# K and V tiles of 2 MB with two kv heads, one on each half of the partitions, in place of 1 MB tiles with one head

## The chip, the cores and the metric

One core of one Trainium2 chip runs one launch of the kernel. The metric is the device time of that launch in microseconds (us). The four runs of the kernel before lie within 0.2% (403.78 to 404.50 us). Where runs of one kernel differ by more than 1.5%, the slower ones count as "slow" and are not compared with fast ones.

## The reference

It is one decode step of a transformer block, batch 4. Layer norm and a query projection come first. Then attention of 32 query heads over the last 4,096 positions of a cache with 16 kv heads, an output projection, and a gated feed-forward layer. All arrays are bf16.

```
W = 4096                                            # the window, of Sk = 16384
q = layernorm(x) @ wq                               # 4 x 32 heads x 128
k, v = k_cache[:, :, Sk-W:, :], v_cache[:, :, Sk-W:, :]     # 4 x 16 x 4096 x 128
p = softmax(q k^T / sqrt(128));  o = p v
h = x + o @ wo
gate = layernorm(h) @ W_gate;  up = layernorm(h) @ W_up
out = h + (relu(gate) * up) @ W_down
```

K and V of the windows are 2 x 4 x 16 x 1 MiB = 134.2 MB. The weights add 25 MB. So the kernel reads about 160 MB and has little arithmetic for it. One head's window is 1 MiB without a gap, and the next head's window starts 4 MiB further on (16,384 x 128 x 2 bytes).

## The kernel before

A tile is one head's window of K or V, 128 partitions x 8 KB: partition p holds 32 successive positions. All large transfers go through one queue, issued by SyncE, into 16 slots. A slot is loaded again when the last reader of its tile is done.

```python
def add_kv(kind, i):
    b, kvh = divmod(i, KVH)
    s = ring_slot()
    off = slot0 + s * TILE
    src = (A_k_cache if kind == "K" else A_v_cache)[b, kvh, SK - WIN:SK, :].rearrange("(p t) d -> p (t d)", p=128)
    place((kind, i), off, TILE, ("TR", i) if kind == "K" else ("PV", i),
          lambda e: e.dma_start(out=arena[:, off:off + TILE], in_=src), key=f"slot{s}")
```

PE transposes each K tile (32 transposes, L373), VectorE and ScalarE copy it out of PSUM, and PE multiplies it with q (L402). After 16 heads come the exponential and the transposes of P (8, L425). Then each V tile is multiplied with P (L452). The P of each head stands in its own columns of `pTm`, with zeros beside it.

Of the kernel before, what the change touches and what calls it, by code (L numbers as in the profile page):

```python
# [11 lines left out]
B = 4  # L12
D = 576
H = 32
KVH = 16
# [4 lines left out]
DC = 5  # L20
NPAIR = B * KVH
SCALE = DH ** -0.5
EPS = 1e-5

NKT = 3
NSLOT = 16
TILE = 4096
QLAG = 2
VDMA_LAG = KVH + 2
PV_LAG = KVH + 3  # L30
# [90 lines left out]
def bass_sequential_preLN__sliding_block_cached__glu_gated_reglu__decode_kernel(  # L121
# [12 lines left out]
    with ExitStack() as es:  # L134
# [11 lines left out]

        arena = sb("arena", [128, (NKT + NSLOT) * TILE], BF16)
        pTm = sb("pTm", [128, 8, 4, KVH, 32], BF16)
        ident_b = sb("ident_b", [128, 128], BF16)
# [33 lines left out]

        kT = [arena[:, i * TILE:(i + 1) * TILE] for i in range(NKT)]
        slot0 = NKT * TILE

# [24 lines left out]

        ring = [(-DC - 2 * NPAIR) % NSLOT]

        def ring_slot():
            s = ring[0] % NSLOT
            ring[0] += 1
            return s

        def add_kv(kind, i):
            b, kvh = divmod(i, KVH)  # L220
            s = ring_slot()
            off = slot0 + s * TILE
            src = (A_k_cache if kind == "K" else A_v_cache)[b, kvh, SK - WIN:SK, :].rearrange("(p t) d -> p (t d)", p=128)
            place((kind, i), off, TILE, ("TR", i) if kind == "K" else ("PV", i),
                  lambda e: e.dma_start(out=arena[:, off:off + TILE], in_=src), key=f"slot{s}")  # L225

        def add_wq(c):
            s = ring_slot()
            off = slot0 + s * TILE
            w = _dw(c)  # L230
            place(("wq", c), off, TILE, "QMM",
                  lambda e: e.dma_start(out=arena[0:w, off:off + H * DH], in_=A_wq[c * 128:c * 128 + w, :]), key=f"slot{s}")  # L232

        P.dma("scalar", ("L", "x"), lambda e: e.dma_start(out=x_bf[:, :], in_=A_x.rearrange("b s d -> (b s) d")), "d_x")
        for s in range(2):
            add_kv("K", s)
        for c in range(DC):
            add_wq(c)
        for s in range(2, NPAIR):
            add_kv("K", s)  # L240
            if s >= VDMA_LAG:
                add_kv("V", s - VDMA_LAG)
        for i in range(NKT):
            for blk in range(i * TILE // 64, (i + 1) * TILE // 64):
                owner[blk] = "QKEND"
# [3 lines left out]
        WDJ = 9 * D  # L249
        rest = list(range(NPAIR - VDMA_LAG, NPAIR))  # L250
        for n, v in enumerate(rest):
            add_kv("V", v)
            if n == len(rest) - 7:
                place(("wo",), WO_OFF, H * D, "WO",
                      lambda e: e.dma_start(out=arena[:, WO_OFF:WO_OFF + H * D].rearrange("p (h n) -> p h n", n=D),
                                            in_=A_wo.rearrange("(h p) n -> p h n", p=128)))
# [16 lines left out]
        def kv(kind, i):  # L273
            off = land[(kind, i)]
            return arena[:, off:off + TILE].rearrange("p (t d) -> p t d", d=DH)
# [38 lines left out]

        tpv = bankb[6]

        def pe_q():
            for c in range(DC):
                w = _dw(c)
                pe(None, lambda e, c=c, w=w: e.transpose(out=tpv[0:w, c * 4:(c + 1) * 4], in_=xn_bf[0:B, c * 128:c * 128 + w],  # L320
                                                         identity=ident_b[0:B, 0:B]), ["xn", "c_idb"] if c == 0 else [])
# [4 lines left out]
            for c in range(DC):  # L326
                w = _dw(c)
                off = land[("wq", c)]
                for n in range(8):
                    g, bk = n % 4, n // 4  # L330
                    pe("QMM", lambda e, c=c, w=w, off=off, n=n, g=g, bk=bk: e.matmul(  # L331
                        bank[4 + bk][32 * g:32 * g + 32, :], lhsT=xnT[0:w, c, :], rhs=arena[0:w, off + n * 512:off + (n + 1) * 512],
                        start=(c == 0), stop=(c == DC - 1), skip_group_check=True),
                        ([("L", "wq", c)] + (["xnT", "c_xnT"] if c == 0 else [])) if n == 0 else [])
            for bk in range(2):
# [24 lines left out]
        def pe_tr(i):  # L360
            kn = kv("K", i)
            for j in range(4):
                for u in range(8):
                    t = j * 8 + u
                    deps = []
                    if u == 0:
                        deps = [("L", "K", i)] if j == 0 else []
                        if i == 0:
                            deps.append("c_idb")
                        else:  # L370
                            deps.append(("EV", i - 1, j))
# [17 lines left out]
        def pe_qk(i):  # L389
            b, kvh = divmod(i, KVH)  # L390
            k = kT[i % NKT]
            for u in range(2):
                for j in range(4):
                    deps = []
                    if u == 0:
                        deps.append(("EV", i, j))
                    if j == 0 and kvh == 0:
                        if b == 0:
                            deps += ["qTm", "qev0", "qev1"]
                        else:  # L400
                            deps += [("EXP", b - 1), ("MAX", b - 1)]
                    o = pe(("QK", i), lambda e, u=u, j=j: e.matmul(  # L402
                        bank[4 + u][32 * j:32 * j + 32, :], lhsT=qTm[:, b, kvh, :],
                        rhs=k[:, j * 1024 + u * 512:j * 1024 + (u + 1) * 512],
                        start=(kvh == 0), stop=(kvh == KVH - 1), skip_group_check=True), deps)
            if i == NPAIR - 1:
                P.names["QKEND"] = o
# [7 lines left out]
        def act_exp(b):  # L415
            act(("EXP", b), lambda e: e.activation(out=p_sb[:, :], in_=s_ps, func=ACT.Exp, bias=stat[:, b, 1:2], scale=SCALE,  # L416
                                                   accum_out=stat[:, b, 2:3]),
                [("NB", b), ("PT", b - 1) if b else ("QT", 7)])

        def pe_pt(b):  # L420
            for tl in range(8):
                deps = []
                if tl == 0:
                    deps = [("EXP", b), ("ONORM", b - 1) if b else "qTm"]
                pe(("PT", b), lambda e, tl=tl: e.transpose(out=mb_ps[:, tl * 128:(tl + 1) * 128],  # L425
                                                           in_=p_sb[:, tl * 128:(tl + 1) * 128], identity=ident_b[:, :]), deps)

        def put_pT(b):
            for half in range(2):
                dst = bass.AP(tensor=pTm, offset=half * 4 * 4 * KVH * 32,  # L430
                              ap=[[8 * 4 * KVH * 32, 128], [KVH * 32, 16], [34, KVH], [1, 2]])
                src = mb_ps[:, half * 512:(half + 1) * 512].rearrange("p (a k h) -> p a k h", k=KVH, h=2)
                deps = [("PT", b), "c_pTm"]
                if b:
                    deps.append(("PV", b * KVH - 1))
                if half == 0:
                    dve(("PM", b, 0), lambda e, dst=dst, src=src: e.tensor_copy(out=dst, in_=src), deps)
                else:
                    dve(("PM", b, 1), lambda e, dst=dst, src=src: e.tensor_copy(out=dst, in_=src), deps)

        def pe_pv(i):
            b, kvh = divmod(i, KVH)
            v = kv("V", i)
            for tl in range(8):
                for j in range(4):
                    deps = []
                    if tl == 0 and j == 0:
                        deps.append(("L", "V", i))
                        if kvh == 0:
                            deps += [("PM", b, 0), ("PM", b, 1)]  # L450
                            deps.append(("OEV", b - 1) if b else "xT")
                    pe(("PV", i), lambda e, tl=tl, j=j: e.matmul(  # L452
                        o_ps[32 * j:32 * j + 32, 0:DH], lhsT=pTm[:, tl, j, kvh, :], rhs=v[:, 8 * j + tl, :],
                        start=(kvh == 0 and tl == 0), stop=(kvh == KVH - 1 and tl == 7), skip_group_check=True), deps)


        def weights(b):
            pe(("MT", b), lambda e: e.matmul(m_ps[0:1, 0:128], lhsT=stat[:, b, 0:1], rhs=ident_f[:, :], start=True, stop=True),
               [("MAX", b), ("PM", b, 0), ("PM", b, 1), "c_idf"])
            dve(("GM", b), lambda e: e.tensor_reduce(out=gm4[0:1, 0:32], in_=m_ps[0:1, 0:128].rearrange("p (j h) -> p h j", j=4),  # L460
# [23 lines left out]
        for s in range(NPAIR + PV_LAG):  # L484
            if s >= PV_LAG and (s - PV_LAG) % KVH == 0:
                pe_pt((s - PV_LAG) // KVH)
                put_pT((s - PV_LAG) // KVH)
            if s < NPAIR:
                pe_tr(s)
                for j in range(4):  # L490
                    evac(s, j)
            if s == 1:
                pe_q()
# [137 lines left out]
```

## Time and profile before

| | before |
|---|---|
| time, median of 4 runs | 404.08 us (403.78 to 404.50) |
| K and V bytes | 134.2 MB in 128 transfers of 1 MB |
| rate while K and V stream | 419 GB/s |
| PE, VectorE, ScalarE busy | 66%, 30%, 34% |

These are lines of the profile's page of the kernel before. First come the span and the engines' busy time in us, with the share of the span and the instructions. Then rows of the span in 40 equal slices (busy tenths, and GB/s). Part 3 has a row for each DMA queue: packets, MB and share of 16 engines. Part 4 is the chain of waits that ended last. The L lines give busy us, mean ns of one, and idle time before them with what ended it. The last lines give count, KB and us from issue to landing.

```profile
span 402.3 us, 10840 instructions
...
PE 265.4 (66%) x5091; PEld 209.7 (52%) x5091; DVE 121.9 (30%) x218; ACT 138.3 (34%) x154; POOL 3.9 (1%) x21
...
DMA  8999999999999999999999999999999999999992
GB/s 321 372 402 422 419 419 419 419 418 421 419 418 421 419 420 419 421 419 418 419 420 419 420 419 420 416 421 419 421 419 419 412 367 370 425 422 415 209 360 118
...
## 3 DMA queue, kind: packets, MB, share of 16 engines
q1 hardware_dynamic: 25104, 159.59, 98.2%
...
q10 hardware_dynamic: 24, 0.01, 0.0%
...
## 4 chain that ended last, share of the span: by engine, by line
DMA 67%; PE 19%; SPq 9%; DVE 3%; issue 1%; ACT 0%
...
L373 PE MATMUL psb<-sb_ident_b,sb_arena 128*128 128x128 bf16 x2048 | 151.9, 243 | 60.4 <-DMA sb_arena<-in_A_k_cache_dram 53.8
...
L452 PE MATMUL psb<-sb_arena,sb_pTm 128*32 128x128 bf16 x2048 | 49.2, 251 | 32.7 <-DMA sb_arena<-in_A_v_cache_dram 31.5
...
sb_arena<-in_A_k_cache_dram SPq DMA_DIRECT2D x64, 1024.0 KB, 27.9
sb_arena<-in_A_v_cache_dram SPq DMA_DIRECT2D x64, 1024.0 KB, 27.6
```

The DMA row is full in nearly every slice, and the GB/s row stays near 419. The two PE groups spend their idle time waiting for K and V transfers. So the data queue is the limit, and PE (66% busy) follows it.

A transfer of n rows here makes n packets for its data and, as the counts below come out, one more for each DMA engine that took part (an inference; no view names the engines). In the packet records of the trace file, which no view lists, these extra packets have 4 bytes: 2,389 of them in this kernel. Queue q10 moved x and half of the output: three transfers of 4 rows, 24 packets. That is 3 x (4 + 4), so four engines took part in each. On q1, 25,104 is the sum over all its transfers if each large one is counted with 16 engines and each of the two outputs with 4 (K and V: 128 x (128 + 16) = 18,432; all others 6,672). The column "DMA share", which a view by windows gives as the mean busy share of the core's 16 engines, bears this reading out for K and V: in the stretch shown below it is 1.01. Texts call the extra packets completions.

The stretch from 40 to 305 us, from the view by windows (us; busy us of PE, PE's weight loads, VectorE, ScalarE and GpSimd; granted clock; DMA share; GB/s):

```profile
core 0: us, PE busy (x) PEld busy (x) DVE busy (x) ACT busy (x) POOL busy (x), PEclk, DMA share, GB/s
40.00:305.00 265.00, 205.63 (x4015) 168.30 (x4016) 97.54 (x162) 122.41 (x131) 0.00 (x0) 0.88 1.01 419
```

And two V tiles from the end of the V stage, in the timeline (start us, duration us, what, and in brackets the idle time before and what ended it). Tiles of 1 MB come 2.48 us apart:

```profile
348.73 1.04 PE L452 MATMUL psb<-sb_arena,sb_pTm 128*32 128x128 bf16 x32 [1.44 <-DMA sb_arena<-in_A_v_cache_dram]
351.21 1.05 PE L452 MATMUL psb<-sb_arena,sb_pTm 128*32 128x128 bf16 x32 [1.44 <-DMA sb_arena<-in_A_v_cache_dram]
```

### The profile page before, as it was taken

The numbers are of one execution on the slowest core, as the hardware profiler recorded it, in microseconds if no ns is written. First come the engines' busy times: TensorE is split into PE (matmuls) and PEld (weight loads), VectorE is DVE, ScalarE is ACT, GpSimd is POOL, SyncE is SP. The second block draws the span as 40 slices with busy tenths as digits, with TensorE's granted clock in tenths as the row PEclk, the third lists the DMA queues.
The fourth block names the chain that finished last, engine by engine and source line by source line (L and its number), as shares of the span: only waits on it lengthen the run. The fifth ranks groups of instructions, "written<-read, shape, count | busy, mean of one in ns | idle before, by whom it ended". The sixth has DMA issues, their size and how long they took to land.

```text
span 402.3 us, 10840 instructions
## 1 busy us (share of the span) xinstructions
PE 265.4 (66%) x5091; PEld 209.7 (52%) x5091; DVE 121.9 (30%) x218; ACT 138.3 (34%) x154; POOL 3.9 (1%) x21
## 2 busy tenths in 40 slices
PE   4555999988777776867776767877774420465253
PEld 4244777766566655656564656666653320342022
DVE  4147555643222243422222433322232000011020
ACT  4222777754333353434333532533330100000010
POOL 3000000000000000000000000000000000000000
PEclk9866999999888889888889897988886555566556
DMA  8999999999999999999999999999999999999992
GB/s 321 372 402 422 419 419 419 419 418 421 419 418 421 419 420 419 421 419 418 419 420 419 420 419 420 416 421 419 421 419 419 412 367 370 425 422 415 209 360 118
DMA packets 25172, 160.29 MB, mean 398 GB/s; under 512 B 2404, under 2 KB 6504, under 8 KB 6504
## 3 DMA queue, kind: packets, MB, share of 16 engines
q1 hardware_dynamic: 25104, 159.59, 98.2%
q8 instruction: 40, 0.66, 0.7%
q10 hardware_dynamic: 24, 0.01, 0.0%
q14 instruction: 4, 0.03, 0.0%
HBM read 159.58 MB, written 0.00 MB: 397 GB/s over the span
## 4 chain that ended last, share of the span: by engine, by line
DMA 67%; PE 19%; SPq 9%; DVE 3%; issue 1%; ACT 0%
DMA sb_arena<-in_A_k_cache_dram 42%; PE psb L373 13%; DMA sb_arena<-in_A_v_cache_dram 11%; DMA sb_arena<-in_B_W_down_dram 10%; SPq L225 8%; DMA sb_arena<-in_A_wq_dram 4%; PE psb L402 3%; DVE sb_pTm L496 2%; PE psb L452 1%; PE psb L518 1%; SPq L232 1%; PE psb L593 0%; DVE sb_stat L410 0%; ACT sb_p_sb L416 0%; PE psb L331 0%
## 5 line engine op out<-in xcount | busy, mean ns | idle before, releaser
L373 PE MATMUL psb<-sb_ident_b,sb_arena 128*128 128x128 bf16 x2048 | 151.9, 243 | 60.4 <-DMA sb_arena<-in_A_k_cache_dram 53.8
L373 PEld LDWEIGHTS psb<-sb_ident_b,sb_arena 128*128 128x128 bf16 x2048 | 140.1, 111 | 74.2 <-DMA sb_arena<-in_A_k_cache_dram 60.2
L387 ACT COPY sb_arena<-psb 128x1024 bf16<-128x1024 bf16 x128 | 125.4, 1014 | 143.2 <-PE psb L373 143.2
L385 DVE COPY sb_arena<-psb 128x1024 bf16<-128x1024 bf16 x128 | 87.9, 690 | 152.0 <-PE psb L373 151.7
L452 PE MATMUL psb<-sb_arena,sb_pTm 128*32 128x128 bf16 x2048 | 49.2, 251 | 32.7 <-DMA sb_arena<-in_A_v_cache_dram 31.5
L452 PEld LDWEIGHTS psb<-sb_arena,sb_pTm 128*32 128x32 bf16 x2048 | 41.6, 113 | 50.7 <-DMA sb_arena<-in_A_v_cache_dram 35.5
L402 PE MATMUL psb<-sb_arena,sb_qTm 128*32 128x512 bf16 x512 | 44.0, 425 | 1.0 <-ACT sb_p_sb L416 1.0
L560 PE MATMUL psb<-sb_arena,sb_hnT 128*32 128x384 bf16 (+1 forms) x120 | 10.2, 500 | 14.8 <-DMA sb_arena<-in_B_W_up_dram 8.4
L523 ACT COPY sb_pTm<-psb 128x288 f32<-128x288 f32 x1 | 0.4, 398 | 46.4 <-PE psb L518 46.4
L478 DVE COPY sb_o_sb<-psb 128x128 f32<-128x128 f32 x4 | 1.2, 291 | 45.2 <-PE psb L452 45.2
L560 PEld LDWEIGHTS psb<-sb_arena,sb_hnT 128*32 128x32 bf16 (+1 forms) x120 | 4.0, 130 | 20.4 <-DMA sb_arena<-in_B_W_up_dram 10.4
L402 PEld LDWEIGHTS psb<-sb_arena,sb_qTm 128*32 128x32 bf16 x512 | 8.1, 97 | 9.0 <-issue 3.3
L564 ACT ACTIVATE sb_pTm<-psb 128x384 f32<-128x384 f32 x3 | 1.3, 492 | 23.9 <-PE psb L560 23.9
L567 DVE TENSOR_TENSOR sb_pTm<-psb,sb_pTm 128x384 bf16<-128x384 f32 x3 | 1.5, 550 | 24.0 <-ACT sb_pTm L564 24.0
L331 PE MATMUL psb<-sb_arena,sb_xnT 128*32 128x512 bf16 (+1 forms) x40 | 3.9, 478 | 6.8 <-DMA sb_arena<-in_A_wq_dram 6.4
L496 DVE MEMSET sb_pTm<- 128x8192 uint32 x1 | 6.9, 6885 | 1.6 <-issue 1.6
L593 PE MATMUL psb<-sb_arena,sb_pTm 128*32 128x144 bf16 x144 | 3.9, 277 | 4.2 <-DMA sb_arena<-in_B_W_down_dram 4.2
L416 ACT ACTIVATE sb_p_sb<-psb,sb_stat 128x1024 bf16<-128x1024 f32 x4 | 4.5, 1114 | 6.2 <-DVE sb_stat L412 6.2
L410 DVE TENSOR_REDUCE sb_stat<-psb 128x1 f32<-128x1024 f32 x4 | 4.9, 1225 | 4.3 <-PE psb L402 4.3
L468 ACT ACTIVATE sb_stat<-sb_stat 128x1 f32<-128x1 f32 x4 | 0.8, 203 | 14.5 <-DVE sb_stat L466 14.5
L593 PEld LDWEIGHTS psb<-sb_arena,sb_pTm 128*32 128x32 bf16 x144 | 3.2, 121 | 4.8 <-DMA sb_arena<-in_B_W_down_dram 4.6
L331 PEld LDWEIGHTS psb<-sb_arena,sb_xnT 128*32 128x32 bf16 (+1 forms) x40 | 0.7, 99 | 9.2 <-DMA sb_arena<-in_A_wq_dram 8.7
(94 smaller groups left out, 64.7 us busy)
## 6 DMA issues: line engine op xcount, KB each, us to landing
sb_arena<-in_A_k_cache_dram SPq DMA_DIRECT2D x64, 1024.0 KB, 27.9
sb_arena<-in_A_v_cache_dram SPq DMA_DIRECT2D x64, 1024.0 KB, 27.6
sb_arena<-in_B_W_down_dram SPq DMA_DIRECT2D x4, 1296.0 KB, 36.5
sb_arena<-in_A_wo_dram SPq DMA_DIRECT2D x1, 4608.0 KB, 31.7
sb_arena<-in_B_W_gate_dram SPq DMA_DIRECT2D x4, 1152.0 KB, 27.0
sb_arena<-in_B_W_up_dram SPq DMA_DIRECT2D x4, 1152.0 KB, 28.4
sb_arena<-in_A_wq_dram SPq DMA_DIRECT2D x4, 1024.0 KB, 11.2
sb_arena<-in_B_W_gate_dram SPq DMA_DIRECT2D x1, 576.0 KB, 33.5
```

Of the source, the lines that this page charges most:

```text
L225: lambda e: e.dma_start(out=arena[:, off:off + TILE], in_=src), key=f"slot{s}")
L331: pe("QMM", lambda e, c=c, w=w, off=off, n=n, g=g, bk=bk: e.matmul(bank[4 + bk][32 * g:32 * g + 32, :], lhsT=xnT[0:w, c, :], rhs=arena[0:w ...
L373: o = pe(("TRJ", i, j), lambda e, j=j, u=u, t=t: e.transpose(out=bankb[TRB[j]][:, u * 128:(u + 1) * 128], in_=kn[:, t, :], identity=ident_ ...
L385: dve(("EV", i, j), lambda e: e.tensor_copy(out=dst, in_=src), deps)
L387: act(("EV", i, j), lambda e: e.copy(out=dst, in_=src), deps)
L402: o = pe(("QK", i), lambda e, u=u, j=j: e.matmul(bank[4 + u][32 * j:32 * j + 32, :], lhsT=qTm[:, b, kvh, :], rhs=k[:, j * 1024 + u * 512:j ...
L410: dve(("MAX", b), lambda e: e.tensor_reduce(out=stat[:, b, 0:1], in_=s_ps, axis=AX.X, op=ALU.max, negate=True), [("QK", b * KVH + KVH - 1)])
L416: act(("EXP", b), lambda e: e.activation(out=p_sb[:, :], in_=s_ps, func=ACT.Exp, bias=stat[:, b, 1:2], scale=SCALE, accum_out=stat[:, b, 2 ...
L452: pe(("PV", i), lambda e, tl=tl, j=j: e.matmul(o_ps[32 * j:32 * j + 32, 0:DH], lhsT=pTm[:, tl, j, kvh, :], rhs=v[:, 8 * j + tl, :], start= ...
L496: dve("c_pTm", lambda e: e.memset(pflat, 0.0))
L560: pe(("GU", c), lambda e, c=c, w=w, g=g, m=m, j=j, lo=lo: e.matmul(bank[3 * g + m][32 * j:32 * j + 32, 0:384], lhsT=hnT[0:w, c, :], rhs=ar ...
L593: pe("DOWN", lambda e, j=j, r=r, n=n, wv=wv: e.matmul(bank[0][32 * n:32 * n + 32, 0:144], lhsT=hhT[:, r * 128 + 32 * j:r * 128 + 32 * j + 32],
```

## The change

The intent: longer runs in memory (16 KB in place of 8 KB), half as many transfers and completions. A tile of 2 MB holds two heads. Head 0 lies on partitions 0 to 63, head 1 on 64 to 127, each with 64 positions (16 KB) per partition. P must then lie on both halves: it is transposed twice, and each half keeps only its head's columns. The wq chunks move to 2 MB tiles as well. Its core, with cuts marked:

```diff
-NSLOT = 16
-TILE = 4096
+NSLOT = 8
+TILE = 8192
...
         def add_kv(kind, i):
-            b, kvh = divmod(i, KVH)
+            b, k2 = divmod(i, BT)
...
-            src = (A_k_cache if kind == "K" else A_v_cache)[b, kvh, SK - WIN:SK, :].rearrange("(p t) d -> p (t d)", p=128)
+            cache = A_k_cache if kind == "K" else A_v_cache
+            src = cache[b, 2 * k2:2 * k2 + 2, SK - WIN:SK, :].rearrange("a (p t) d -> a p (t d)", p=64)
...
-                        rhs=k[:, j * 1024 + u * 512:j * 1024 + (u + 1) * 512],
+                        bank[4 + u][32 * j:32 * j + 32, :], lhsT=qTm[:, b, 2 * k2 + a, :], rhs=k[:, j, :, a, :],
...
-                pe(("PT", b), lambda e, tl=tl: e.transpose(out=mb_ps[:, tl * 128:(tl + 1) * 128],
-                                                           in_=p_sb[:, tl * 128:(tl + 1) * 128], identity=ident_b[:, :]), deps)
+                for a in range(2):
+                    pe(("PT", b, r), lambda e, tl=tl, a=a: e.transpose(out=mb_ps[64 * a:64 * a + 64, tl * 128:(tl + 1) * 128],
+                                                                       in_=p_sb[:, (r * 8 + tl) * 64:(r * 8 + tl + 1) * 64],
+                                                                       identity=ident_b[:, :]), deps if a == 0 else [])
...
+            for a in range(2):
+                dst = bass.AP(tensor=pTm, offset=64 * a * 16384 + r * 8192 + 2 * a, ap=[[16384, 64], [256, 32], [36, BT], [1, 2]])
```

More of the change, by code (lines that the diff above doesn't have):

```diff
@@ L21 @@
 NPAIR = B * KVH
+NTILE = NPAIR // 2
+BT = KVH // 2
 SCALE = DH ** -0.5
@@ L25 @@
 NKT = 3
-NSLOT = 16
-TILE = 4096
+NSLOT = 8
+TILE = 8192
+UNIT = 4096
 QLAG = 2
-VDMA_LAG = KVH + 2
+VDMA_LAG = BT + 1
 PV_LAG = KVH + 3
@@ L144, in bass_sequential_preLN__sliding_block_cached__glu_gated_reglu__decode_kernel @@
         pool = lambda name, fn, deps=(): P.op("gpsimd", name, fn, deps)
-        arena = sb("arena", [128, (NKT + NSLOT) * TILE], BF16)
-        pTm = sb("pTm", [128, 8, 4, KVH, 32], BF16)
+        arena = sb("arena", [128, NKT * UNIT + NSLOT * TILE], BF16)
+        pTm = sb("pTm", [128, 16, 4, BT, 32], BF16)
         ident_b = sb("ident_b", [128, 128], BF16)
@@ L182, in bass_sequential_preLN__sliding_block_cached__glu_gated_reglu__decode_kernel @@
         hhT = pflat[:, 4608:4608 + 1152]
-        kT = [arena[:, i * TILE:(i + 1) * TILE] for i in range(NKT)]
-        slot0 = NKT * TILE
+        kT = [arena[:, i * UNIT:(i + 1) * UNIT] for i in range(NKT)]
+        slot0 = NKT * UNIT
         psb = es.enter_context(nc.psum_tensor("psb", [128, 8, 512], FP32))
@@ L210, in place @@
             land[name] = off
-        ring = [(-DC - 2 * NPAIR) % NSLOT]
+        ring = [(-3 - 2 * NTILE) % NSLOT]
         def ring_slot():
@@ L219, in add_kv, with add_wq @@
         def add_kv(kind, i):
-            b, kvh = divmod(i, KVH)
+            b, k2 = divmod(i, BT)
             s = ring_slot()
             off = slot0 + s * TILE
-            src = (A_k_cache if kind == "K" else A_v_cache)[b, kvh, SK - WIN:SK, :].rearrange("(p t) d -> p (t d)", p=128)
-            place((kind, i), off, TILE, ("TR", i) if kind == "K" else ("PV", i),
+            cache = A_k_cache if kind == "K" else A_v_cache
+            src = cache[b, 2 * k2:2 * k2 + 2, SK - WIN:SK, :].rearrange("a (p t) d -> a p (t d)", p=64)
+            place((kind, i), off, TILE, ("TR", 2 * i + 1) if kind == "K" else ("PV", 2 * i + 1),
                   lambda e: e.dma_start(out=arena[:, off:off + TILE], in_=src), key=f"slot{s}")
-        def add_wq(c):
+        wq_off = []
+        def add_wq(m):
             s = ring_slot()
             off = slot0 + s * TILE
-            w = _dw(c)
-            place(("wq", c), off, TILE, "QMM",
-                  lambda e: e.dma_start(out=arena[0:w, off:off + H * DH], in_=A_wq[c * 128:c * 128 + w, :]), key=f"slot{s}")
-        P.dma("scalar", ("L", "x"), lambda e: e.dma_start(out=x_bf[:, :], in_=A_x.rearrange("b s d -> (b s) d")), "d_x")
-        for s in range(2):
-            add_kv("K", s)
-        for c in range(DC):
-            add_wq(c)
-        for s in range(2, NPAIR):
+            if m < 2:
+                wq_off.extend([off, off + H * DH])
+                src = A_wq[m * 256:(m + 1) * 256, :].rearrange("(p r) n -> p (r n)", r=2)
+                place(("wq", m), off, TILE, "QMM", lambda e: e.dma_start(out=arena[:, off:off + TILE], in_=src), key=f"slot{s}")
+            else:
+                wq_off.append(off)
+                place(("wq", m), off, TILE, "QMM",
+                      lambda e: e.dma_start(out=arena[0:64, off:off + H * DH], in_=A_wq[512:576, :]), key=f"slot{s}")
+        P.dma("scalar", ("L", "x"), lambda e: e.dma_start(out=x_bf[:, :], in_=A_x.rearrange("b s d -> (b s) d")), "d_x")
+        add_kv("K", 0)
+        for m in range(3):
+            add_wq(m)
+        for s in range(1, NTILE):
             add_kv("K", s)
@@ L243, in bass_sequential_preLN__sliding_block_cached__glu_gated_reglu__decode_kernel @@
         for i in range(NKT):
-            for blk in range(i * TILE // 64, (i + 1) * TILE // 64):
+            for blk in range(i * UNIT // 64, (i + 1) * UNIT // 64):
                 owner[blk] = "QKEND"
@@ L249, in bass_sequential_preLN__sliding_block_cached__glu_gated_reglu__decode_kernel @@
         WDJ = 9 * D
-        rest = list(range(NPAIR - VDMA_LAG, NPAIR))
+        rest = list(range(NTILE - VDMA_LAG, NTILE))
         for n, v in enumerate(rest):
             add_kv("V", v)
-            if n == len(rest) - 7:
+            if n == len(rest) - 4:
                 place(("wo",), WO_OFF, H * D, "WO",
@@ L273, in kv @@
         def kv(kind, i):
-            off = land[(kind, i)]
+            off = land[(kind, i // 2)]
             return arena[:, off:off + TILE].rearrange("p (t d) -> p t d", d=DH)
@@ L315, in bass_sequential_preLN__sliding_block_cached__glu_gated_reglu__decode_kernel @@
         tpv = bankb[6]
+        xn_rows = lambda c: (xn_bf[0:B, 512:576] if c == 4 else
+                             xn_bf[0:B, c // 2 * 256:c // 2 * 256 + 256].rearrange("b (p r) -> b r p", r=2)[:, c % 2, :])
         def pe_q():
@@ L319, in pe_q @@
                 w = _dw(c)
-                pe(None, lambda e, c=c, w=w: e.transpose(out=tpv[0:w, c * 4:(c + 1) * 4], in_=xn_bf[0:B, c * 128:c * 128 + w],
+                pe(None, lambda e, c=c, w=w: e.transpose(out=tpv[0:w, c * 4:(c + 1) * 4], in_=xn_rows(c),
                                                          identity=ident_b[0:B, 0:B]), ["xn", "c_idb"] if c == 0 else [])
@@ L327, in pe_q @@
                 w = _dw(c)
-                off = land[("wq", c)]
+                off = wq_off[c]
                 for n in range(8):
@@ L333, in pe_q @@
                         start=(c == 0), stop=(c == DC - 1), skip_group_check=True),
-                        ([("L", "wq", c)] + (["xnT", "c_xnT"] if c == 0 else [])) if n == 0 else [])
+                        ([("L", "wq", c // 2)] + (["xnT", "c_xnT"] if c == 0 else [])) if n == 0 and c % 2 == 0 else [])
             for bk in range(2):
@@ L363, in pe_tr @@
                 for u in range(8):
-                    t = j * 8 + u
+                    t = j * 16 + i % 2 * 8 + u
                     deps = []
                     if u == 0:
-                        deps = [("L", "K", i)] if j == 0 else []
+                        deps = [("L", "K", i // 2)] if j == 0 else []
                         if i == 0:
@@ L389, in pe_qk @@
         def pe_qk(i):
-            b, kvh = divmod(i, KVH)
-            k = kT[i % NKT]
-            for u in range(2):
+            dp, u = divmod(i, 2)
+            b, k2 = divmod(dp, BT)
+            k = kT[i % NKT].rearrange("p (j t a k) -> p j t a k", j=4, t=8, a=2)
+            for a in range(2):
                 for j in range(4):
                     deps = []
-                    if u == 0:
+                    if a == 0:
                         deps.append(("EV", i, j))
-                    if j == 0 and kvh == 0:
+                    if j == 0 and k2 == 0:
                         if b == 0:
@@ L401, in pe_qk @@
                             deps += [("EXP", b - 1), ("MAX", b - 1)]
-                    o = pe(("QK", i), lambda e, u=u, j=j: e.matmul(
-                        bank[4 + u][32 * j:32 * j + 32, :], lhsT=qTm[:, b, kvh, :],
-                        rhs=k[:, j * 1024 + u * 512:j * 1024 + (u + 1) * 512],
-                        start=(kvh == 0), stop=(kvh == KVH - 1), skip_group_check=True), deps)
+                    o = pe(("QK", i), lambda e, a=a, j=j: e.matmul(
+                        bank[4 + u][32 * j:32 * j + 32, :], lhsT=qTm[:, b, 2 * k2 + a, :], rhs=k[:, j, :, a, :],
+                        start=(k2 == 0 and a == 0), stop=(k2 == BT - 1 and a == 1), skip_group_check=True), deps)
             if i == NPAIR - 1:
@@ L417, in act_exp, with pe_pt @@
                                                    accum_out=stat[:, b, 2:3]),
-                [("NB", b), ("PT", b - 1) if b else ("QT", 7)])
-        def pe_pt(b):
+                [("NB", b), ("PT", b - 1, 1) if b else ("QT", 7)])
+        def pe_pt(b, r):
             for tl in range(8):
@@ L423, in pe_pt, with put_pT @@
                 if tl == 0:
-                    deps = [("EXP", b), ("ONORM", b - 1) if b else "qTm"]
-                pe(("PT", b), lambda e, tl=tl: e.transpose(out=mb_ps[:, tl * 128:(tl + 1) * 128],
-                                                           in_=p_sb[:, tl * 128:(tl + 1) * 128], identity=ident_b[:, :]), deps)
-        def put_pT(b):
-            for half in range(2):
-                dst = bass.AP(tensor=pTm, offset=half * 4 * 4 * KVH * 32,
-                              ap=[[8 * 4 * KVH * 32, 128], [KVH * 32, 16], [34, KVH], [1, 2]])
-                src = mb_ps[:, half * 512:(half + 1) * 512].rearrange("p (a k h) -> p a k h", k=KVH, h=2)
-                deps = [("PT", b), "c_pTm"]
+                    deps = [("PM", b, 0, 0), ("PM", b, 0, 1)] if r else [("EXP", b), ("ONORM", b - 1) if b else "qTm"]
+                for a in range(2):
+                    pe(("PT", b, r), lambda e, tl=tl, a=a: e.transpose(out=mb_ps[64 * a:64 * a + 64, tl * 128:(tl + 1) * 128],
+                                                                       in_=p_sb[:, (r * 8 + tl) * 64:(r * 8 + tl + 1) * 64],
+                                                                       identity=ident_b[:, :]), deps if a == 0 else [])
+        def put_pT(b, r):
+            for a in range(2):
+                dst = bass.AP(tensor=pTm, offset=64 * a * 16384 + r * 8192 + 2 * a, ap=[[16384, 64], [256, 32], [36, BT], [1, 2]])
+                src = mb_ps[64 * a:64 * a + 64, :].rearrange("p (m q a h) -> p m q a h", q=BT, a=2, h=2)[:, :, :, a, :]
+                deps = [("PT", b, r), "c_pTm"]
                 if b:
                     deps.append(("PV", b * KVH - 1))
-                if half == 0:
-                    dve(("PM", b, 0), lambda e, dst=dst, src=src: e.tensor_copy(out=dst, in_=src), deps)
+                if a == 0:
+                    dve(("PM", b, r, a), lambda e, dst=dst, src=src: e.tensor_copy(out=dst, in_=src), deps)
                 else:
-                    dve(("PM", b, 1), lambda e, dst=dst, src=src: e.tensor_copy(out=dst, in_=src), deps)
+                    act(("PM", b, r, a), lambda e, dst=dst, src=src: e.copy(out=dst, in_=src), deps)
         def pe_pv(i):
-            b, kvh = divmod(i, KVH)
+            dp, u = divmod(i, 2)
+            b, k2 = divmod(dp, BT)
             v = kv("V", i)
@@ L447, in pe_pv @@
                     if tl == 0 and j == 0:
-                        deps.append(("L", "V", i))
-                        if kvh == 0:
-                            deps += [("PM", b, 0), ("PM", b, 1)]
+                        deps.append(("L", "V", dp))
+                        if k2 == 0 and u == 0:
+                            deps += [("PM", b, r, a) for r in range(2) for a in range(2)]
                             deps.append(("OEV", b - 1) if b else "xT")
                     pe(("PV", i), lambda e, tl=tl, j=j: e.matmul(
-                        o_ps[32 * j:32 * j + 32, 0:DH], lhsT=pTm[:, tl, j, kvh, :], rhs=v[:, 8 * j + tl, :],
-                        start=(kvh == 0 and tl == 0), stop=(kvh == KVH - 1 and tl == 7), skip_group_check=True), deps)
+                        o_ps[32 * j:32 * j + 32, 0:DH], lhsT=pTm[:, u * 8 + tl, j, k2, :], rhs=v[:, 16 * j + 8 * u + tl, :],
+                        start=(k2 == 0 and u == 0 and tl == 0), stop=(k2 == BT - 1 and u == 1 and tl == 7),
+                        skip_group_check=True), deps)
         def weights(b):
             pe(("MT", b), lambda e: e.matmul(m_ps[0:1, 0:128], lhsT=stat[:, b, 0:1], rhs=ident_f[:, :], start=True, stop=True),
-               [("MAX", b), ("PM", b, 0), ("PM", b, 1), "c_idf"])
+               [("MAX", b), ("PM", b, 1, 0), ("PM", b, 1, 1), "c_idf"])
             dve(("GM", b), lambda e: e.tensor_reduce(out=gm4[0:1, 0:32], in_=m_ps[0:1, 0:128].rearrange("p (j h) -> p h j", j=4),
@@ L485, in bass_sequential_preLN__sliding_block_cached__glu_gated_reglu__decode_kernel @@
             if s >= PV_LAG and (s - PV_LAG) % KVH == 0:
-                pe_pt((s - PV_LAG) // KVH)
-                put_pT((s - PV_LAG) // KVH)
+                pe_pt((s - PV_LAG) // KVH, 0)
+                put_pT((s - PV_LAG) // KVH, 0)
             if s < NPAIR:
@@ L491, in bass_sequential_preLN__sliding_block_cached__glu_gated_reglu__decode_kernel @@
                     evac(s, j)
+            if s >= PV_LAG and (s - PV_LAG) % KVH == 0:
+                pe_pt((s - PV_LAG) // KVH, 1)
+                put_pT((s - PV_LAG) // KVH, 1)
             if s == 1:
```

## The prediction

> **What bounds the kernel now.** The data queue. In the profile's 40 slices the DMA row is full at about 419 GB/s from 40 to 305 us, while PE is 66% busy, ScalarE 34%, VectorE 30%. The chain that ended last is 67% DMA. K and V alone are 134.2 MB: 320 us of the 402 at that rate. The rest hides behind it, except start and tail.
>
> **What the change intends.** Runs of 16 KB instead of 8 KB, half as many transfers. In the trace's packets an 8 KB run takes 309 to 312 ns, one of 9 KB 348, one of 10,368 B 389. The slope gives 610 ns for 16 KB (estimate): under 2% better than two of 8 KB. Extra PE work (24 more transposes of P per batch, 2 to 3 us), a copy moved to ScalarE and K columns read with a stride stay inside idle time. Alone: 400 to 407 us.
>
> **What I think it does instead.** The source of each K/V transfer now has dimensions 2 heads x 64 x 16 KB; the slowest has two entries. [...] Destination 128, source 2: two engines. [...] The scalar queue moved three transfers of four rows (x, two outputs) in 24 packets: 12 rows + 12 completions, four engines each, not 16. And the main queue's 25,104 packets come out exactly when every large transfer is counted with 16 completions and the two small outputs with 4.
>
> Then one head (64 runs of 16 KB) goes through one engine: 64 x 610 ns = 39.0 us per 2 MB tile, about 53 GB/s in all instead of 419. Tiles queue on the same two engines:
> - 64 tiles x 39.05 us = 2,499 us
> - their share of wq: 11 us
> - their share of wo, gate/up and down[...]: 13 + 25 + 12.5 = about 51 us
> - start, last matmuls, output: 6 us
>
> Sum 2,567 us, all on the critical path: compute per tile (about 5 us of PE) is far below 39 us. With eight slots the two engines should never run dry.
>
> **Predicted: 2,567 us, range 2,480 to 2,680.** Faster by over 2%: 0.02. Within 2%: 0.08. Slower: 0.90.
>
> **What would show it.**
> - Mean bandwidth near 62 GB/s; the 40 slices show DMA share near 1 tenth and 53 GB/s nearly throughout.
> - Main queue packets 14,704 (64 tiles x (128+2) and the rest), not 15,600 (64 x (128+16)).
> - K and V landing 270 to 320 us after issue (eight tiles in flight), against 28 now.
> - The chain over 95% DMA on K and V; PE busy near 10%.
> - From the last V to the end about 45 to 50 us, as now.
>
> **What would make it wrong.** If the lowering leaves 64 or 128 slowest in the source, 16 engines take part: 15,600 packets, 400 to 410 us. With four or eight engines: about 1,300 or 690 us. If a lone engine is faster than one of sixteen (309 ns against 312 hints at little), time scales with the 16 KB packet: 590 ns would give 2,485.

"Two engines": no trace had shown it for two heads, so that step was an assumption. What supported it is in the trace of the kernel before: the packets of three transfers of 4 rows, by which four engines carried each. The sum: 2,499 + 11 + 51 + 6 = 2,567 us, all worked out from packet times of the trace of the kernel before, but for the 6.

## The result

| | before | changed |
|---|---|---|
| time, median of 4 runs | 404.08 us | 2,608.45 us (2,607.47 to 2,609.44) |
| ratio | | 6.455 (95% interval 6.444 to 6.466) |
| mean rate over the span | 398 GB/s | 62 GB/s |
| main queue packets | 25,104 | 14,704 |

A ratio is the mean time of one kernel's fast runs over that of the other's of the same rounds, so it is not quite the ratio of the medians quoted.

The same lines of the changed kernel's page:

```profile
span 2605.7 us, 10945 instructions
...
PE 314.3 (12%) x5187; PEld 246.5 (9%) x5187; DVE 123.2 (5%) x218; ACT 144.1 (6%) x162; POOL 4.0 (0%) x21
...
DMA  3111111111111111111111111111111111113145
GB/s 108 54 54 54 54 54 54 54 54 54 54 54 54 54 54 54 54 54 54 54 54 54 54 54 54 54 54 54 54 54 54 54 54 54 54 54 111 67 124 158
...
## 3 DMA queue, kind: packets, MB, share of 16 engines
q1 hardware_dynamic: 14704, 159.58, 15.8%
...
q10 hardware_dynamic: 24, 0.01, 0.0%
...
## 4 chain that ended last, share of the span: by engine, by line
another core or an unknown queue 85%; PE 11%; DMA 3%; DVE 0%; issue 0%; ACT 0%; SPq 0%
...
L387 PE MATMUL psb<-sb_ident_b,sb_arena 128*128 128x128 bf16 x2048 | 176.9, 266 | 1167.4 <-DMA sb_arena<-in_A_k_cache_dram 1167.4
...
L469 PE MATMUL psb<-sb_arena,sb_pTm 128*32 128x128 bf16 x2048 | 58.7, 288 | 1088.0 <-DMA sb_arena<-in_A_v_cache_dram 1088.0
...
sb_arena<-in_A_k_cache_dram SPq DMA_DIRECT2D x32, 2048.0 KB
sb_arena<-in_A_v_cache_dram SPq DMA_DIRECT2D x32, 2048.0 KB
```

The bytes are the same, 160 MB, but the GB/s row reads 54 from the second slice on and the DMA row stands at 1 tenth. PE waits 1,167 us for K and 1,088 us for V, 87% of the span together. The packets are 14,704 = 64 x (128 + 2) + 6,384: two engines took part in each K and V transfer. With 16 it would be 64 x (128 + 16) + 6,384 = 15,600. The packets of 4 bytes went from 2,389 to 437.

The chain of waits fails here: "another core or an unknown queue" stands where the page before named K and V. That label is no sign of few engines: split and heads16 below show it too (31% and 36%), with 16 engines and landings 62 and 68 us after issue. The landing times of K and V are missing too, as in every run here with fewer than 16 engines in a K or V transfer. The waits of PE, which are read from PE's own records, still name the transfers.

The long middle stretch, by windows (columns as before, here and below):

```profile
60.00:2340.00 2280.00, 274.75 (x4414) 219.48 (x4414) 112.37 (x184) 134.88 (x147) 0.00 (x0) 0.55 0.13 54
```

A DMA share of 0.13 is two engines of sixteen. And two V tiles in the timeline, of 2 MB each:

```profile
2245.61 1.90 PE L469 MATMUL psb<-sb_arena,sb_pTm 128*32 128x128 bf16 x64 [32.66 <-DMA sb_arena<-in_A_v_cache_dram]
2284.57 1.04 PE L469 MATMUL psb<-sb_arena,sb_pTm 128*32 128x128 bf16 x32 [37.07 <-DMA sb_arena<-in_A_v_cache_dram]
...
```

They come 38.96 us apart, where 2 MB took 2 x 2.48 = 4.96 us before. In the trace's packet records a 16 KB packet takes 611 ns (median), and 64 of them are 39.1 us: this fits one head on each engine, one row after the other. All transposes of P together (L441) take 6.2 us of PE and do not matter beside this.

### The profile page after: what moved, and what is told of

Read it like the earlier page. It is cut to its first block, busy times and chain, and to the rows that moved or that the text cites. A ratio compares the mean times of both kernels' runs of the same rounds, so it can differ in the third digit from the quotient of the medians.

```text
span 2605.7 us, 10945 instructions
## 1 busy us (share of the span) xinstructions
PE 314.3 (12%) x5187; PEld 246.5 (9%) x5187; DVE 123.2 (5%) x218; ACT 144.1 (6%) x162; POOL 4.0 (0%) x21
## 3 DMA queue, kind: packets, MB, share of 16 engines
q1 hardware_dynamic: 14704, 159.58, 15.8%
## 4 chain that ended last, share of the span: by engine, by line
another core or an unknown queue 85%; PE 11%; DMA 3%; DVE 0%; issue 0%; ACT 0%; SPq 0%
PE psb L387 7%; PE psb L469 2%; DMA sb_arena<-in_A_k_cache_dram 2%; PE psb L417 2%; DMA sb_arena<-in_B_W_down_dram 1%; PE psb L441 0%; PE psb L345 0%; PE psb L539 0%; PE psb L491 0%; PE psb L482 0%; PE psb L497 0%; PE psb L476 0%; PE psb L614 0%; PE psb L547 0%
## 5 line engine op out<-in xcount | busy, mean ns | idle before, releaser
L387 PE MATMUL psb<-sb_ident_b,sb_arena 128*128 128x128 bf16 x2048 | 176.9, 266 | 1167.4 <-DMA sb_arena<-in_A_k_cache_dram 1167.4
L387 PEld LDWEIGHTS psb<-sb_ident_b,sb_arena 128*128 128x128 bf16 x2048 | 164.1, 123 | 1185.0 <-DMA sb_arena<-in_A_k_cache_dram 1177.0
L469 PE MATMUL psb<-sb_arena,sb_pTm 128*32 128x128 bf16 x2048 | 58.7, 288 | 1088.0 <-DMA sb_arena<-in_A_v_cache_dram 1088.0
L441 PE MATMUL psb<-sb_ident_b,sb_p_sb 128*64 128x128 bf16 x128 | 6.2, 250 | 2.0 <-DVE sb_oT L499 1.3
L441 PEld LDWEIGHTS psb<-sb_ident_b,sb_p_sb 128*64 128x64 bf16 x128 | 4.8, 128 | 3.7 <-issue 1.4
## 6 DMA issues: line engine op xcount, KB each, us to landing
sb_arena<-in_B_W_up_dram SPq DMA_DIRECT2D x4, 1152.0 KB, 56.5
```

Source lines behind the costliest of these rows:

```text
L387: o = pe(("TRJ", i, j), lambda e, j=j, u=u, t=t: e.transpose(out=bankb[TRB[j]][:, u * 128:(u + 1) * 128], in_=kn[:, t, :], identity=ident_ ...
L441: pe(("PT", b, r), lambda e, tl=tl, a=a: e.transpose(out=mb_ps[64 * a:64 * a + 64, tl * 128:(tl + 1) * 128], in_=p_sb[:, (r * 8 + tl) * 64 ...
L469: pe(("PV", i), lambda e, tl=tl, j=j: e.matmul(o_ps[32 * j:32 * j + 32, 0:DH], lhsT=pTm[:, u * 8 + tl, j, k2, :], rhs=v[:, 16 * j + 8 * u ...
```

## The experiments

Theory: the source of the transfer lists the two heads as its slowest dimension, so two engines carry it. Rivals: the new run length or tile size is slow; the new compute is slow; two streams 4 MiB apart in memory collide.

Kernels with a single run: the losses that are read from them are far larger than the spread among the runs of one kernel here, which is at most 2%, but for split (637 to 693 us, 9%).

The correctness test on the chip does not tell much here. Scores of these inputs are small and the softmax is nearly flat, so a kernel with K and V rows on wrong partitions still passed.

### before_two: two engines in the kernel before

```diff
-src = (A_k_cache if kind == "K" else A_v_cache)[b, kvh, SK - WIN:SK, :].rearrange("(p t) d -> p (t d)", p=128)
+g, h = divmod(kvh, 2)
+lo = SK - WIN + h * 2048
+src = (A_k_cache if kind == "K" else A_v_cache)[b, 2 * g:2 * g + 2, lo:lo + 2048, :].rearrange("a (p t) d -> a p (t d)", p=64)
```

> The kernel before, its tiles of 1 MB and runs of 8 KB and all its compute kept; only each K/V transfer reads half a window of two heads, 2 x 64 x 8 KB, instead of one whole head. Wrong numbers on purpose. Engine-count theory: two engines, 8,192 packets of about 309 ns on each: 2,531 us plus about 75 us of weights, start and end = 2,570 to 2,650 us; main queue packets 128 x (128+2) + 6,672 = 23,312. If run length, tile size or the P work of the change is the cause: about 404 us.

Measured: 2,635.39 us (one run). Two lines of its page:

```profile
GB/s 106 54 54 54 53 53 53 54 54 54 54 53 54 54 53 54 54 53 54 54 54 54 54 54 54 54 54 54 54 54 54 54 53 54 54 54 110 52 121 173
...
q1 hardware_dynamic: 23312, 159.58, 15.8%
```

Run length, tile size and all compute are those of the kernel before, and the time is within 1.1% of the changed kernel's. The packets are 23,312 as expected. So the new source alone brings the loss, without the longer runs or the P work. It changes two things, though: the slowest dimension has two entries, and two heads are read at once. The next run separates them.

### swapped: the order of the source's dimensions

```diff
-src = cache[b, 2 * k2:2 * k2 + 2, SK - WIN:SK, :].rearrange("a (p t) d -> a p (t d)", p=64)
+src = cache[b, 2 * k2:2 * k2 + 2, SK - WIN:SK, :].rearrange("a (p t) d -> p a (t d)", p=64)
```

> The changed kernel, still one 2 MB transfer per tile, only the order of the source's dimensions turned round: 64 x 2 heads x 16 KB. Wrong numbers on purpose (rows land on other partitions); same bytes, same runs, same instructions. Engine-count theory: slowest dimension 64 against 128, so 16 engines: 398 to 412 us, 15,600 packets. Rival 'two streams 4 MiB apart in memory collide' [...]

Measured: 398.29 us (398.12 to 398.64), ratio to before 0.986 (0.984 to 0.987), 15,600 packets.

```profile
GB/s 316 384 408 423 422 425 426 427 428 425 422 427 425 425 425 427 432 423 425 423 423 428 430 425 425 424 427 425 425 423 428 414 374 368 426 424 419 230 360 139
...
q1 hardware_dynamic: 15600, 159.59, 97.6%
```

The same bytes, in the same 2 MB transfers and 16 KB runs, with the same instructions around them, take 398 us when 64 comes first. Here too both heads, 4 MiB apart, are read at once, at 426 GB/s (mean from 40 to 305 us). So the memory rival falls for two streams.

### split: one transfer per head

```diff
-place((kind, i), off, TILE, reader, lambda e: e.dma_start(out=arena[:, off:off + TILE], in_=src), key=f"slot{s}")
+for a in range(2):
+    src = cache[b, 2 * k2 + a, SK - WIN:SK, :].rearrange("(p t) d -> p (t d)", p=64)
+    P.dma("sync", ("L", kind, i), lambda e, a=a, src=src: e.dma_start(
+        out=arena[64 * a:64 * a + 64, off:off + TILE], in_=src), f"slot{s}", deps if a == 0 else [])
```

(The removed line is shortened.)

> The changed kernel with each 2 MB transfer cut into two, one per head, onto 64 partitions each. All else of the change stays (16 KB runs, both-halves P, strided K columns). Engine-count theory: the slowest source dimension is 64, so 16 engines take part again: 398 to 410 us, main queue packets 64 x 2 x (64+16) + 6,384 = 16,624, K and V at about 420 GB/s. Rival 'the new compute is the brake': still about 2,600 us. Rival '16 KB runs are slow': well above 404 us. Whether it beats the kernel before is open: 0.99 to 1.01 of it.

Measured: 677.38 us, median of six runs from 637 to 693, too scattered for a ratio. The page below is of a run of 654 us. Even the fastest takes 1.58 times the kernel before. The packets are 16,624 as expected, so 16 engines took part, and yet the expectation of 398 to 410 us missed by far.

```profile
DMA  8999999999999999999999999999999999899991
GB/s 244 289 210 212 216 210 221 229 229 221 224 219 223 224 224 224 232 227 236 232 233 243 248 253 267 255 279 271 282 286 306 313 307 229 231 211 299 386 312 67
...
q1 hardware_dynamic: 16624, 159.59, 97.4%
```

The DMA row is full, but at about 220 GB/s for the first half, about half of the 426 of swapped, rising to 313 later; a 16 KB packet took 1,153 ns (median) in place of 611. The engines are busy and each is slow. Counting engines is not enough.

### heads16: sixteen heads in one transfer

```diff
+n, r = 16, 128 // 16
+g, h = divmod(k2, n // 2)
+lo = SK - WIN + h * r * 64
+src = cache[b, n * g:n * g + n, lo:lo + r * 64, :].rearrange("a (p t) d -> a p (t d)", p=r)
```

> One 2 MB transfer per tile from 16 heads, 8 runs of 16 KB from each; source dimensions 16 x 8 x 16 KB. Wrong numbers on purpose, same bytes and instructions. Engine-count theory: [...]16 engines: 398 to 412 us, 15,600 packets. Rival 'heads 4 MiB apart collide'[...].

Measured: 680.69 us (677 to 690, of which 690 counts as slow), fast runs 1.684 times those of before (1.676 to 1.692), 15,600 packets.

```profile
GB/s 227 279 215 217 215 219 217 221 216 227 220 219 219 224 225 226 223 218 217 230 235 247 254 239 232 230 234 248 270 296 296 261 237 220 203 212 250 417 297 135
...
q1 hardware_dynamic: 15600, 159.59, 97.4%
```

Again 16 engines and little over half the rate (234 GB/s from 40 to 560 us), and again my expectation missed. With the split it asks for a second theory.

In the split, each transfer writes 64 partitions, 0 to 63 or 64 to 127, where swapped's (426 GB/s) wrote all 128. So my guess was that the rate depends on which partitions the sixteen engines write at one time. A transfer of heads16 covers all 128 partitions; the guess would reach it only by the order in which the engines write, and the packet records do not name engines, so for heads16 it was not shown. The next two runs test the guess on 64 partitions. The expectations call it the port theory.

### port_0 and port_32: the same transfers onto other partitions

Every head is its own transfer of 64 rows. Both heads of a tile go to the same 64 partitions, in two column ranges of a slot of double width; four slots. The two kernels differ in one number. Their outputs are wrong, which doesn't matter for the times.

```diff
 P.dma("sync", ("L", kind, i), lambda e, a=a, src=src: e.dma_start(
-    out=arena[0:0 + 64, off + a * HALF:off + a * HALF + HALF], in_=src), ...      # port_0
+    out=arena[32:32 + 64, off + a * HALF:off + a * HALF + HALF], in_=src), ...    # port_32
```

> Port theory (why the split and the 16-head run took 677 and 681 us though 16 engines took part)[...]. The changed kernel with every head as its own transfer of 64 rows of 16 KB, all to partitions 0 to 63 (the second head to another column range; 4 slots; wrong numbers on purpose). [...] Expected: 16 KB packets of about 1,150 ns, 640 to 760 us. Rival 'a transfer of 64 rows is slow by itself': the same here as in port_32.

> As port_0, one number changed: all heads go to partitions 32 to 95[...]. Port theory: 16 KB packets of about 611 to 640 ns, 400 to 470 us (four slots instead of eight may leave gaps). Rival 'a transfer of 64 rows is slow by itself', or 'half-tile transfers pay per transfer': same as port_0.

Measured: port_0 743.36 us, port_32 416.10 us (one run each, same chip). By windows, port_0 and then port_32:

```profile
100.00:600.00 500.00, 220.12 (x3699) 176.15 (x3700) 85.36 (x141) 109.58 (x120) 0.00 (x0) 0.68 1.01 207
```

```profile
40.00:300.00 260.00, 200.51 (x3845) 163.94 (x3843) 102.06 (x158) 123.45 (x134) 0.00 (x0) 0.87 1.00 414
```

With one start partition changed, the rate goes from 207 to 414 GB/s, and the median 16 KB packet from 1,275 to 611 ns. Both have a DMA share of 1, so on partitions 0 to 63 the engines are as busy and each packet takes twice as long. A transfer of 64 rows is not slow by itself, and both kernels read the same addresses in the same order, so memory cannot explain the pair. So it matters which 64 partitions are written; why, the pair does not show. port_32 also shows that slots are hardly a brake: half of them, and still 416 us.

### heads4 and heads8: four and eight engines

The edit is that of heads16 with n = 4 and n = 8.

> One 2 MB transfer per tile from 4 heads, 32 runs of 16 KB each: source 4 x 32 x 16 KB, wrong numbers on purpose. Four engines: packets 64 x (128+4) + 6,384 = 14,832. By the engine count alone, as in the prediction: about 1,300 us and packets of 611 ns. [...]

> One 2 MB transfer per tile from 8 heads, 16 runs of 16 KB each, wrong numbers on purpose: 8 engines, 64 x (128+8) + 6,384 = 15,088 packets. By the count of engines: K and V in 625 us, 680 to 700 us in all. [...]

Measured: heads4 1,402.42 us, heads8 892.45 us (one run each), packets 14,832 and 15,088 as expected. Two lines of the page of heads4, then of heads8:

```profile
GB/s 149 87 102 108 107 109 107 109 108 109 108 109 108 109 108 109 108 108 108 109 108 109 108 109 108 109 107 108 108 108 108 109 108 108 176 117 87 169 204 134
...
q1 hardware_dynamic: 14832, 159.58, 30.4%
```

```profile
GB/s 146 168 115 118 125 129 142 155 152 158 194 213 214 218 207 181 202 218 216 216 215 194 186 212 215 218 214 206 185 196 140 161 209 123 111 197 161 193 277 100
...
q1 hardware_dynamic: 15088, 159.59, 55.5%
```

The number of engines sets the ceiling: the steady rate is 54 GB/s with two, 108 with four, and up to 218 with eight. Estimates from packet times: for heads4 up to 2,600 us if packets took about 1,200 ns, twice the 611 of the changed kernel (64 x 32 x 1.2 = 2,458 us for K and V, and the rest on top); for heads8 690 to 740 us if packets came down to 612 ns as in heads4 (64 x 16 x 0.612 = 627), and 1,250 to 1,350 if they stayed near the 1,120 of heads16 (1,147). heads8 took 892 us, between these two and 30% above the count alone. It needs about a quarter of its span to get there. In its packet records a 16 KB packet takes 1,166 ns on average from 50 to 60 us, after wq has landed, 612 from 260 to 300 us, and later more again. In heads4 it takes 744 ns from 60 to 70 us and 613 from 90 us on. (The packets before that prove nothing: the 256 packets of wq, also of 16 KB, run among them on 16 engines, and the changed kernel is slow there too, with 893 ns over the first 24th of these packets.) heads16 never got there: its 24ths stay between 857 and 1,228 ns, 1,121 on average. That the partitions written are the cause in these three runs is not shown: they read 4, 8 and 16 heads at once, 4 MiB apart, so memory stays a rival here. Why the packets become fast in one case and not in another, no run shows.

### weights_late: what the sum in the prediction lacked

```diff
-            if n == len(rest) - 4:
+            if n == len(rest) - 1:
                 place(("wo",), ...)
+                P.names[("L", "wo")].deps.append(("PV", NPAIR - 1))
```

> What my sum lacked (2,567 predicted, 2,608 measured). Theory: while transfers on all 16 engines (wo, gate/up) move, the V packets of 16 KB on the two engines take 850 to 1,160 ns in place of 612; counted against the steady 131 packets in 40 us, V lost about 29 us near the end (7 at wo, 21 at gate/up), besides 13 us for wo's own share. Here wo, gate/up and down start only after the last V has been used, all else as changed. Expected: V packets stay at 612 ns to the end, the last V's matmuls at about 2,517 us of the span instead of 2,559, then 49 us of weights: 2,565 to 2,590 us, faster than the changed kernel although nothing overlaps. Rival 'the time lies elsewhere (issue, gaps between tiles)': last V at about 2,545 and a total of 2,595 to 2,625.

Measured: 2,583.53 us (2,582.66 to 2,584.58), 25 us less than the changed kernel although the weights now overlap nothing. The last two V tiles, in the changed kernel and then here:

```profile
2502.75 1.90 PE L469 MATMUL psb<-sb_arena,sb_pTm 128*32 128x128 bf16 x64 [39.03 <-DMA sb_arena<-in_A_v_cache_dram]
2559.29 1.90 PE L469 MATMUL psb<-sb_arena,sb_pTm 128*32 128x128 bf16 x64 [54.64 <-DMA sb_arena<-in_A_v_cache_dram]
```

```profile
2479.67 1.90 PE L470 MATMUL psb<-sb_arena,sb_pTm 128*32 128x128 bf16 x64 [37.08 <-DMA sb_arena<-in_A_v_cache_dram]
2518.63 1.90 PE L470 MATMUL psb<-sb_arena,sb_pTm 128*32 128x128 bf16 x64 [37.07 <-DMA sb_arena<-in_A_v_cache_dram]
```

The last V is used at 2,518.6 us, expected 2,517, against 2,559.3; and the tiles stay 38.96 us apart to the end. In the changed kernel, V tiles were up to 56.5 us apart while the weights moved. In its packet records V packets, 612 ns each when nothing else moved, took 762 to 1,021 ns on average in steps of 10 us from 2,500 us on. So transfers on 16 engines slow the two that carry V. The rival expected 2,545 and falls. Where the weights and V meet, this run does not show.

### interleaved: 16 engines, 2 MB tiles and a right result

The two heads lie on alternate partitions. Each column of P is written twice, one transpose covers both heads, and a 0/1 column masks by head. Cuts are marked, and a few dependency changes are left out.

```diff
-src = cache[b, 2 * k2:2 * k2 + 2, SK - WIN:SK, :].rearrange("a (p t) d -> a p (t d)", p=64)
+src = cache[b, 2 * k2:2 * k2 + 2, SK - WIN:SK, :].rearrange("a (p t) d -> p a (t d)", p=64)
...
-k = kT[i % NKT].rearrange("p (j t a k) -> p j t a k", j=4, t=8, a=2)
+k = kT[i % NKT].rearrange("p (j t k a) -> p j t a k", j=4, t=8, a=2)
...
+twice = bass.AP(tensor=p_sb, offset=0, ap=[[1024, 128], [1, 1024], [0, 2]])
+dve(("P2", b), lambda e: e.tensor_copy(out=p2[:, :].rearrange("p (k a) -> p k a", a=2), in_=twice), ...)
...
+dve(("PM", b, r, a), lambda e, dst=dst, src=src, a=a: e.tensor_scalar(
+    out=dst, in0=src, scalar1=par[:, a:a + 1], scalar2=None, op0=ALU.mult), deps)
```

> One 2 MB transfer per tile on 16 engines that computes the right result: source order 64 x 2 heads x 16 KB, so the two heads lie on alternate partitions. K columns read with a stride of two elements; each column of P written twice, one transpose per position, and VectorE multiplies by a 0/1 column to mask by head. Expected as the swapped order measured: 396 to 401 us, 0.98 to 0.99 of the kernel before, 15,600 packets. If the strided K reads or the extra VectorE work reach the critical path: 402 to 410.

Measured: 398.62 us (398.50 to 400.43), ratio 0.987 (0.985 to 0.989): 1.3% less than the kernel before, clear of 1, though it is under 2%. In the same stretch as shown for the kernel before:

```profile
40.00:305.00 265.00, 203.69 (x4063) 165.65 (x4064) 107.42 (x175) 122.18 (x131) 0.00 (x0) 0.89 1.01 425
```

425 GB/s against 419 is the whole gain that the change was after. In the packet records 16 KB takes 619 ns on average, and two of 8 KB took 2 x 317 = 633. VectorE's busy time rises from 97.5 to 107.4 us and stays hidden. Since the chip's test is blind to misplaced rows, I also computed this kernel with K, V, wq and wo scaled up until the softmax had peaks, in a simulation of values, not of times: its relative error was 0.0046, as for the kernel before. The swapped order had 1.02. (The same simulation with other scales gave 0.0051, 0.0052 for the kernel before, and 1.07.)

## Why the prediction was right

- **The step that decides was right.** The split of a K or V transfer followed the slowest dimension of its source here: by the packets, 2, 4, 8 or 16 entries gave as many engines, and 64 gave 16. (The destination of K and V always had 64 or 128 rows, so whether it counts as well was not tested.) Two engines took part in each K and V transfer: 14,704 packets, as predicted. before_two shows that such a source is enough to bring the loss, and swapped that the order of its dimensions alone is enough to undo it.
- **The largest term was right.** 39.05 us per tile was predicted and 38.96 measured; a 16 KB packet takes 611 ns, where 610 was worked out from 8, 9 and 10 KB packets.
- **The sum was 41 us low** (2,567 against 2,608), inside the range. The missing term is what transfers on 16 engines cost the two engines. In weights_late the last V is used at 2,518.6 us; 64 x 38.96 + 11 for wq + 1 for the start is 2,505, so about 13 us are left over, probably lost beside wq at the start; no run shows where. From there to 2,559.3 in the changed kernel are 41 us: 13 for wo's own share, which I had, and 28 which I had not. From the last V to the end it took 46 us; I had 45 to 50.
- **Wrong in part: "the chain over 95% DMA on K and V".** The view put 85% down to an unknown queue. The step that failed was to trust a view that infers releasers. PE's waits show 87%, and PE's own work, which hides behind the transfers, is 12%.
- **Wrong: "landing 270 to 320 us after issue (eight tiles in flight)".** No view gives the landings, but the trace has SyncE's issues and PE's first use of each tile, for which PE was waiting. From the start of an issue to the use it is 121 us for K and 123 us for V (medians), so about three tiles were in flight. Most issues themselves took 38 us; why, no run shows. It cost nothing here, because a DMA share of 0.13 means that the two engines did not run dry.
- **Wrong in part: "with four or eight engines: about 1,300 or 690 us".** heads4 took 1,402 and heads8 892. The count of engines is only a ceiling. heads4 held it in the middle (tiles 19.5 us apart, 64 x 19.5 = 1,248 us) but by that spacing its second K tile was about 36 us late (used at 82.0 us), and four of its last five V tiles came 27 to 47 us after the one before, while the weights moved. heads8 fell short for much of its span.
- **"400 to 407 us" for 16 engines** was a little high: swapped took 398.3. The rate rose from 419 to 426 GB/s, 1.7%, within the "under 2%" that was worked out from packets, and the time fell by 1.4%.

## What to carry to other kernels

Before merging transfers, write down the dimensions of both sides as they are issued. In every run here the source's slowest one decided how many DMA engines carried a K or V transfer (2, 4, 8 and 16 entries gave as many, 64 and 128 gave 16), and the packets row tells how many did: rows plus one per engine (14,704 packets with two engines, 15,600 with 16). Then ask which partitions the engines write at one time; 64 rows onto partitions 0 to 63 ran at half rate (207 GB/s), and onto 32 to 95 at full rate (414). Where two sources must share a tile, alternate them in the fast dimension and let the compute follow, if it has idle time (interleaved: 425 GB/s, 398.62 us).
